# Weight pieces, chunk 1's twiddle terms and the transform lead in the early part of a fused FFT-filter and MoE kernel

## Chip, cores and metric

One NeuronCore of a Trainium2 chip runs the whole program in one launch. The metric is device time in microseconds (us) of an execution; lower is better. Engine names: PE is TensorE (matmuls), DVE is VectorE, ACT is ScalarE, POOL is GpSimd, SP is the SyncE queue that issues most DMAs.

## Reference

Three layers follow each other over a batch of 8 sequences of 3072 tokens with 256 channels. The spectrum filter acts along the sequence, the other two on each token.

```python
X = np.fft.rfft(x, axis=1); Y = X * (filt_r + 1j * filt_i)[None]
y = np.fft.irfft(Y, n=3072, axis=1)                    # (8, 3072, 256)
h = np.maximum(np.maximum(y @ w1, y @ w2), y @ w3)     # 256 -> 768
x = h @ w_out                                          # 768 -> 256
h = x @ w_in                                           # 256 -> 1024
e = exp(h - max(h)); solu = h * e / (sum(e) + 1e-09)
ln = (solu - mean) / sqrt(var + 1e-06) * g_ln
out = ln @ w_out2
```

## The kernel before

**Transforms.** The 8 sequences and two halves of the channels make 16 chunks (chunk = 2 x sequence + half). A chunk's 24 x 128 transform is a radix part on DVE (`dft8` L274, `fwd3` L337, and on the way back `inv3` L360, `idft8` L303) around four groups of 128-point products on PE (`prod`, L390, fp32). For a group `fwd_in` (L395) multiplies by twiddles into a tile U, `middle` (L444) makes the products in a PSUM pair `pf` and multiplies them by the filter on DVE (Y and M), and `inv_out` (L521) multiplies back, and ACT and DVE scale the result out of `pf` into the chunk's tile S (T by ACT, then `S<-pf,tws,T` by DVE). Chunks 0 to 3 use full products, later ones half products with two partition swaps by DMA. For chunks 0 and 1 (`apart`, L392) the two summands of each twiddle term are not added: ACT makes both, in U and in T, and PE sums them by two more products. For the later chunks ACT makes one summand and DVE adds the other: `stt(U[...], X[...], col("c", k), T[...])`, L419 and L438.

**Tiles.** Chunk tiles go round in five buffers with tags s0 to s4 (`take`, L257: `j = ch % NS`). Two of them first serve the weights: `w3f` holds w3 in tag s2, the buffer of chunk 2 (L142), and `raws` holds three incoming pieces in tag s4, the buffer of chunk 4 (L177).

**Weights of the MoE.** They arrive as float64 bits in 12 pieces (`PIECES`, L172: for each third of d_ff w3, w1, w2, w_out). `moe_weights` (L175) loads a piece by SP (L190), `from_f64` (L151) turns it into fp32 on DVE and ACT, w3 is subtracted from w1 and w2 (L198), and each weight is split in a high and a low part (L199, L200). Behind the last piece come six rounds (L203 to L215, transposes of `w3f` on PE, a copy on ACT, a subtraction on DVE L210, six products) that multiply w3 with w_out into `a_h`, `a_l` (L217, L218); this is called the fold here. They hold two of the four PSUM banks of tag h throughout.

**MoE steps.** A step `moe(i)` (L755) is one block of 128 hidden units for 512 tokens: `up` (L700) makes 12 products in two banks, ACT and DVE take the maximum (L710, L712) and split it (L715, L716), and `down` (L719) of two steps earlier adds 6 products into `o`. Six steps make a group of 512 tokens, closed by 12 products with `a_h`, `a_l` (L736); 36 steps make a sequence. A group's tokens come from the finished transform by a transpose on DVE and 16 SP DMAs (`flip`, L661, tiles yt and zt), then ACT and DVE split them (`xT`, L676, xh and xl). So the first group of a sequence needs both its chunks, and steps 37 and 73 are the first of the second and third sequence.

**What sets the order.** The program is written as generators: the transforms are one stream (`fft_stream`, L625), advanced by `advance()`, and the loop at L791 writes a step and then advances the stream up to a budget of DVE cost:

```python
while cost[0] - c0 < (i + 1) * PACE + LEAD * min(1.0, i / RAMP) and idle < 12:
```

The tile framework's scheduler then orders each engine's instructions from the written order. On the chip each engine runs its instructions in that order, and SP issues its DMAs in that order too, so that a row that waits holds up all rows behind it. The first loop (L773) advances the stream until a third of chunks 0 and 1 is back (Y), with a weight piece at every 20th advance for `EARLY` = 4 pieces; the other eight and the fold are written after step 0 (L794). `fft_stream` writes chunk 4's radix part (L645) only after chunk 3 is complete (L642).

From the seventh sequence on the program needs no transforms any more; the last sequence of the first MoE is mixed with the second MoE's first products, and then the second MoE runs alone to the end.

Of the kernel before, what the change touches and what calls it, by code (L numbers as in the profile page):

```python
# [10 lines left out]
F32 = mybir.dt.float32  # L11
# [8 lines left out]
P = 128  # L20
# [79 lines left out]
def kernel(ctx: ExitStack, tc: tile.TileContext, xr, ff, tw, dft,  # L100
                                 w1, w2, w3, w_out, w_in2, w_out2, g_ln, out):
    nc = tc.nc
    B = xr.shape[0]
    DFF = w1.shape[1]
    NF = DFF // P
# [19 lines left out]
    fc = fx.enter_context(tc.tile_pool(name="fc", bufs=1))  # L125
# [13 lines left out]
    w_h = [wp.tile([P, 2, DFF], F32R, tag=f"w{j}h", name=f"w{j}h") for j in range(2)]  # L139
    w_l = [wp.tile([P, 2, DFF], F32R, tag=f"w{j}l", name=f"w{j}l") for j in range(2)]  # L140

    w3f = fc.tile([P, 2, DFF], F32, tag="s2", name="w3f")  # L142
    a_h = wp.tile([P, 2, D], F32R, tag="ah", name="ah")
    a_l = wp.tile([P, 2, D], F32R, tag="al", name="al")
    wo_h = wp.tile([P, NF, D], F32R, tag="woh", name="woh")
# [5 lines left out]
    def from_f64(raw, e, out=None, eng=nc.gpsimd):  # L151

        lw, hw = raw[:, 0::2], raw[:, 1::2]
        lf, hf, ef = lw.bitcast(F32), hw.bitcast(F32), e.bitcast(F32)
        nc.vector.tensor_scalar(e, hw, 0x7FF00000, None, op0=ALU.bitwise_and)
        nc.scalar.activation(e, e, AF.Relu, bias=ebias, scale=8.0)
        nc.vector.tensor_scalar(lw, lw, 8, None, op0=ALU.logical_shift_right)
        nc.vector.scalar_tensor_tensor(e, hw, -2 ** 31, e, op0=ALU.bitwise_and, op1=ALU.bitwise_or)
        nc.vector.tensor_scalar(hw, hw, 0xFFFFF, None, op0=ALU.bitwise_and)
        nc.scalar.activation(hf, hw, AF.Copy, bias=1.0, scale=2.0 ** -20)  # L160
        nc.vector.scalar_tensor_tensor(lf, lw, 2.0 ** -44, hf, op0=ALU.mult, op1=ALU.add)
        if out is not None:
            ef, lf = (v.rearrange("p (c w) -> p c w", c=2) for v in (ef, lf))
            eng.tensor_tensor(out, ef, lf, op=ALU.mult)
            return e.bitcast(F32)
        eng.tensor_tensor(ef, ef, lf, op=ALU.mult)
        return ef
# [2 lines left out]


    PIECES = [(q, j) for q in range(NF // 2) for j in (2, 0, 1, 3)]  # L172
    EARLY = 4

    def moe_weights():  # L175

        raws = yp.tile([P, 3, 1024], I32, tag="s4", name="raws")  # L177
        for i, (q, j) in enumerate(PIECES):
# [11 lines left out]
            nc.sync.dma_start(raw.rearrange("p (c w) -> p c w", c=2), src.rearrange("(c p) w -> p c w", p=P))  # L190
            with tc.issue_after(GATE[0]) if i >= EARLY else nullcontext():
                v = from_f64(raw, e, w3f[:, :, fs] if j == 2 else None, nc.vector)
# [40 lines left out]
    FULL, SUMS = 4, 2  # L233
# [19 lines left out]
    def free(ch):  # L253

        return ch < NS or ((ch - NS) // 2, TG - 1) in FLIPPED
# [18 lines left out]
    def dft8(ch):  # L274
        take(ch)
        O = S[ch]
        scr = scratch()
        eo, f = by3(scr[:, 0:24]), by3(scr[:, 24:30])
        parts = [slice(a, a + 1) for a in range(3)] if ch == 0 else [slice(0, 3)]
        for a in parts:  # L280
            tt(eo[:, 0:4, a], O[:, 0:4, a], O[:, 4:8, a], ALU.add)
            yield
            tt(eo[:, 4:8, a], O[:, 0:4, a], O[:, 4:8, a], ALU.subtract)
            yield
        tt(f[:, 0:2], eo[:, 0:2], eo[:, 2:4], ALU.add)
        yield
        tt(O[:, 6:8], eo[:, 0:2], eo[:, 2:4], ALU.subtract)
        yield
        tt(O[:, 0], f[:, 0], f[:, 1], ALU.add)
        yield  # L290
        tt(O[:, 1], f[:, 0], f[:, 1], ALU.subtract)
        yield
        h = eo[:, 0:2]
        tt(h[:, 0], eo[:, 5], eo[:, 7], ALU.subtract)
        yield
        tt(h[:, 1], eo[:, 5], eo[:, 7], ALU.add)
        yield
        stt(O[:, 2:4], h, C8, eo[:, 4:8:2])
        yield
        stt(O[:, 4:6], h, -C8, eo[:, 4:8:2])  # L300
        yield
# [58 lines left out]
    def inv3(ch):  # L360
        v = S[ch]
        scr = scratch()
        s, d, t, t0 = scr[:, 0:6], scr[:, 6:12], scr[:, 12:18], scr[:, 18:20]
        tt(s, v[:, 2:8, 1], v[:, 2:8, 2], ALU.add)
        yield
        tt(d, v[:, 2:8, 1], v[:, 2:8, 2], ALU.subtract)
        yield
        stt(t, s, -0.5, v[:, 2:8, 0])
        yield
        tt(v[:, 2:8, 0], v[:, 2:8, 0], s, ALU.add)  # L370
        yield
        stt(v[:, 3:8:2, 1], d[:, 0:6:2], H3, t[:, 1:6:2])
        stt(v[:, 2:8:2, 2], d[:, 1:6:2], H3, t[:, 0:6:2])
        yield
        stt(v[:, 2:8:2, 1], d[:, 1:6:2], -H3, t[:, 0:6:2])
        stt(v[:, 3:8:2, 2], d[:, 0:6:2], -H3, t[:, 1:6:2])
        yield
        stt(t0, v[:, 0:2, 1], -0.5, v[:, 0:2, 0])
        tt(v[:, 0:2, 0], v[:, 0:2, 0], v[:, 0:2, 1], ALU.add)
        yield  # L380
        tt(v[:, 0:2, 1], t0, v[:, 0:2, 2], ALU.add)
        tt(v[:, 0:2, 2], t0, v[:, 0:2, 2], ALU.subtract)
        yield
# [6 lines left out]
        nc.tensor.matmul(o, m, rows(src, i0, i1), start=first, stop=last)  # L390

    def apart(ch, g):  # L392
        return ch < SUMS

    def fwd_in(ch, g):  # L395
        sl, ks = GROUPS[g]
# [182 lines left out]
    def together(*gens):  # L579
        gens = [g for g in gens if g is not None]  # L580
        while gens:
            for g in list(gens):
                try:
                    next(g)
                except StopIteration:
                    gens.remove(g)
                else:
                    yield

    def seq(*gens):  # L590
        for g in gens:
            yield from g

    def groups(ch, last=None):

        if last is None:
            yield from fwd_in(ch, 0)
        else:
            yield from together(fwd_in(ch, 0), last)
        yield from together(fwd_in(ch, 1), middle(ch, 0))  # L600
        yield from together(fwd_in(ch, 2), middle(ch, 1), inv_out(ch, 0))
        yield from together(fwd_in(ch, 3), middle(ch, 2), inv_out(ch, 1))

    def rest(ch):
        yield from together(middle(ch, 3), inv_out(ch, 2))
        yield from inv_out(ch, 3)

    def stages(before, ch):

        ready = ch is not None and free(ch)  # L610
        if ready:
            yield from dft8(ch)
        if before is not None:
            while before not in VDONE:
                yield
            yield from inv3(before)
            yield from idft8(before)
        if ch is not None:
            if not ready:
                while not free(ch):  # L620
                    yield
                yield from dft8(ch)
            yield from fwd3(ch)

    def fft_stream():  # L625

        one, two = slice(0, 1), slice(1, 3)
        yield from dft8(0)
        yield from fwd3(0)
        yield from together(groups(0), stages(None, 1))  # L630
        yield from together(groups(1, rest(0)), first(0, one))
        yield from rest(1)
        yield from first(1, one)
        yield from idft8(0, two)
        yield from idft8(1, two)
        last = 2 * B - 1
        if B > 1:

            yield from stages(None, 2)
            yield from together(groups(2), stages(None, 3))  # L640
            yield from together(groups(3, rest(2)), stages(2, None))
            yield from seq(rest(3), inv3(3), idft8(3))  # L642
        for ch in range(4, 2 * B):
            if ch == 4:
                yield from stages(None, 4)  # L645
            yield from together(groups(ch, rest(ch - 1) if ch > 4 else None),
                                stages(ch - 1 if ch > 4 else None, ch + 1 if ch < last else None))
        if B > 2:
            yield from seq(rest(last), inv3(last), idft8(last))

    def first(ch, part):
        while ch not in VDONE:
            yield
        yield from inv3(ch)
        yield from idft8(ch, part)
# [99 lines left out]
    def moe(i):  # L755
        b, tg, f = steps[i]
        up(b, tg, f)
        if i >= LD:
            down(*steps[i - LD])
        j = b * TG + tg + 1  # L760
        if f == XF and j < B * TG:
            xT(*divmod(j, TG))
        if f == FF and j < B * TG:
            have(*divmod(j, TG))
            flip(*divmod(j, TG))

    XF, FF = 4, 1
    wgen = moe_weights()
# [4 lines left out]
    while (0, 0, 0) not in Y or (0, 1, 0) not in Y:  # L773
        advance()
        n += 1
        if n == 1:
            nc.sync.dma_start(tws, tw)
            nc.sync.dma_start(dfull, dft[:, 4:14])
            nc.sync.dma_start(df, dft[:, 0:4])
        if n % NW0 == 0 and n <= EARLY * NW0:  # L780
            next(wgen)
# [4 lines left out]
    xT(0, 0)  # L786
    c0 = cost[0]

    PACE, LEAD, RAMP = 3080.0, 16000.0, 6
    n_a = (B - 1) * per  # L790
    for i in range(n_a):  # L791
        moe(i)
        b, tg, f = steps[i]
        if i == 0:  # L794
            for _ in wgen:
                pass
        idle, at = 0, cost[0]
        while cost[0] - c0 < (i + 1) * PACE + LEAD * min(1.0, i / RAMP) and idle < 12:
            if not advance():
                break  # L800
            idle, at = (0, cost[0]) if cost[0] > at else (idle + 1, at)
# [282 lines left out]
```

## Time and profile before

| | us |
|---|---|
| median of 3 runs (2787.57 to 2789.47) | 2788.5 |
| the profiled execution's own time | 2787.83 |
| its span in the trace | 2786.0 |
| PE busy, share of the span | 2675.1, 96% |
| DVE busy, share of the span | 2308.8, 83% |
| ACT busy | 1485.2, 53% |
| POOL busy | 905.9, 33% |

The profiled execution is 0.7 us below the median. Times in the trace count from the span's start, so 1.8 us of the execution lie around the span. Steps are told here by the start of their L712 on DVE: the n-th L712 is the n-th step.

### The profile page before, as it was taken

The page shows a single profiled execution, that of the slowest core. Times are in us where ns is not written, and L with a number is a line of the kernel's source. Part 1 is how long each engine was busy: PE and PEld are TensorE (multiplying, and loading weights), DVE is VectorE, ACT ScalarE, POOL GpSimd, SP SyncE. Part 2 cuts the span into 40 slices and gives each one's busy share as a digit, 9 for nine tenths or more (in the row PEclk, how much of TensorE's full clock was granted, in tenths as well). Part 3 has the DMA queues.
Part 4 walks back from the last instruction along what each step waited for, and adds up shares of the span by engine and source line. Part 5 has one row for each costly group of instructions (what it writes and reads, how often), then busy time and mean ns, then how long its engine had stood idle before and what let it go on. Part 6 is the DMA issues. An engine that isn't in the chain of part 4 may idle for free.

```text
span 2786.0 us, 37981 instructions
## 1 busy us (share of the span) xinstructions
PE 2675.1 (96%) x12008; PEld 2154.1 (77%) x12008; DVE 2308.8 (83%) x3962; ACT 1485.2 (53%) x2896; POOL 905.9 (33%) x1302
## 2 busy tenths in 40 slices
PE   6779979979999999999999999999999999999999
PEld 3457757757777777777778888888888888888888
DVE  8797699999799898998988635988878878778885
ACT  4244334434444444444434434777777777677775
POOL 0001101101111111111111101666767776766765
PEclk9889989989999999999999999999999999999999
DMA  4123113322323224223322312556555555555543
GB/s 165 40 93 101 37 37 82 114 60 76 104 78 101 83 73 119 61 71 99 84 70 80 95 31 61 145 134 159 143 141 138 144 146 142 150 145 138 144 125 91
DMA packets 162281, 285.58 MB, mean 103 GB/s; under 512 B 34464, under 2 KB 95392, under 8 KB 160160
## 3 DMA queue, kind: packets, MB, share of 16 engines
q1 hardware_dynamic: 121376, 232.82, 31.4%
q10 hardware_dynamic: 40704, 50.35, 5.5%
q8 instruction: 94, 1.54, 0.2%
q14 instruction: 107, 0.88, 0.1%
HBM read 89.04 MB, written 50.33 MB: 50 GB/s over the span
## 4 chain that ended last, share of the span: by engine, by line
PE 79%; DVE 15%; DMA 2%; issue 1%; SPq 1%; ACT 1%; POOL 0%; DVEq 0%; ACTq 0%; POOLq 0%
PE h L707 20%; PE h L885 19%; PE p L954 13%; PE pf L390 7%; PE p L956 7%; DVE scr L240 4%; PE o L736 4%; PE o L728 3%; PE o L729 3%; PE o L727 3%; DVE S L244 2%; DVE S L240 1%; DVE h L712 1%; DVE hl L716 1%; SPq L672 1%
## 5 line engine op out<-in xcount | busy, mean ns | idle before, releaser
L947 POOL TENSOR_TENSOR sl<-zt,sh 128x1024 fp32r<-128x1024 f32 x188 | 452.4, 2406 | 106.1 <-ACT sh L946 99.2
L954 PE MATMUL p<-V,sh 128*128 128x512 f32 x1536 | 380.9, 390 | 0.0
L896 DVE SCALAR_TENSOR_TENSOR sp<-h,e 128x1024 f32<-128x1024 f32 x192 | 234.3, 1220 | 172.1 <-ACT e L894 170.0
L240 POOL TENSOR_TENSOR M<-M,M 128x384 f32<-128x384 f32 (+1 forms) x96 | 134.4, 1420 | 685.0 <-DVE M L240 505.1
L715 ACT CAST hh<-h 128x512 fp32r<-128x512 f32 x288 | 169.3, 589 | 349.4 <-DVE h L712 336.7
L954 PEld LDWEIGHTS p<-V,sh 128*128 128x128 f32 x1536 | 287.5, 188 | 59.5
L710 ACT ACTIVATE hm<-h 128x512 f32<-128x512 f32 x288 | 172.9, 601 | 247.4 <-PE h L707 246.1
L894 ACT ACTIVATE e<-h,sm 128x1024 f32<-128x1024 f32 x192 | 213.7, 1113 | 107.5 <-DVE sm L892 61.4
L946 ACT CAST sh<-zt 128x1024 fp32r<-128x1024 f32 x188 | 196.6, 1047 | 117.9 <-PE p L954 94.3
L892 DVE TENSOR_REDUCE sm<-h 128x1 f32<-128x1024 f32 x192 | 230.9, 1203 | 28.0 <-PE h L885 27.4
L898 ACT ACTIVATE e<-sp,sm 128x1024 f32<-128x1024 f32 x192 | 220.5, 1149 | 55.1 <-DVE sm L900 54.0
L728 PE MATMUL o<-hl,woh 128*128 128x512 f32 x576 | 238.7, 414 | 9.7 <-DVE hl L716 9.4
L885 PE MATMUL h<-wih,x2h 128*128 128x512 f32 x768 | 244.0, 392 | 1.2 <-ACT xo L739 1.2
L712 DVE TENSOR_TENSOR h<-hm,h 128x512 f32<-128x512 f32 x288 | 197.3, 685 | 55.8 <-PE h L707 51.7
L885 PE MATMUL h<-wih,x2l 128*128 128x512 f32 x768 | 241.5, 391 | 0.0
L885 PE MATMUL h<-wil,x2h 128*128 128x512 f32 x768 | 238.2, 390 | 0.0
L913 DVE STREAM_TRANSPOSE yt<-sp 128x1024 f32<-128x1024 f32 x188 | 231.5, 1231 | 5.2 <-issue 1.0
L727 PE MATMUL o<-hh,woh 128*128 128x512 f32 x576 | 231.6, 402 | 3.3 <-ACT hh L715 3.3
L716 DVE TENSOR_TENSOR hl<-h,hh 128x512 fp32r<-128x512 f32 x288 | 195.7, 681 | 41.4 <-ACT hh L715 41.0
L729 PE MATMUL o<-hh,wol 128*128 128x512 f32 x576 | 226.7, 394 | 0.0
L956 PEld LDWEIGHTS p<-V,sl 128*128 128x128 f32 x1536 | 209.8, 190 | 15.0
L956 PE MATMUL p<-V,sl 128*128 128x256 f32 x1536 | 214.7, 282 | 0.0
(160 smaller groups left out, 5757.3 us busy)
## 6 DMA issues: line engine op xcount, KB each, us to landing
zt<-yt SPq DMA_DIRECT2D x752, 128.0 KB, 2.7
x<-xo SPq DMA_DIRECT2D x96, 256.0 KB, 2.2
x<-x ACTq DMA_DIRECT2D x48, 512.0 KB, 3.7
out_dram<-ob ACTq DMA_DIRECT2D x192, 128.0 KB, 2.3
zt<-yt SPq DMA_DIRECT2D x752, 32.0 KB, 1.9
S<-in_xr_dram SPq DMA_DIRECT2D x15, 1536.0 KB, 8.3
F<-in_ff_dram SPq DMA_DIRECT2D x48, 384.0 KB, 3.4
F<-in_ff_dram SPq DMA_DIRECT2D x16, 512.0 KB, 4.2
```

The costliest lines, as they stand in the source:

```text
L240: eng.tensor_tensor(o, a, b, op=op)
L707: nc.tensor.matmul(ph[j], wt[:, c, f * P:(f + 1) * P], xt[:, c], start=i == 0, stop=i == 5)
L727: nc.tensor.matmul(po[m], wo_h[:, f, cs], hh, start=f == 0, stop=False)
L728: nc.tensor.matmul(po[m], wo_h[:, f, cs], hl, start=False, stop=False)
L729: nc.tensor.matmul(po[m], wo_l[:, f, cs], hh, start=False, stop=False)
L885: nc.tensor.matmul(h[:, fs], xt[:, c, ts], wt[:, c, fs], start=n == 0, stop=n == 5)
L892: nc.vector.tensor_reduce(sm[:, 0:1], h, axis=AX.X, op=ALU.max, negate=True)
L896: nc.vector.scalar_tensor_tensor(sp, h, 1.0, e, op0=ALU.mult, op1=ALU.mult, accum_out=sm[:, 2:3])
L913: nc.vector.transpose(out=YT[g][:, :, t].rearrange("p j c k -> p c j k"), in_=sp.rearrange("p (c j k) -> p c j k", c=NF2, j=4))
L947: nc.gpsimd.tensor_tensor(lv, z, hv, op=ALU.subtract)
L954: nc.tensor.matmul(p, sh[:, c], V2[:, c], start=c == 0, stop=False)
L956: nc.tensor.matmul(p[:, :D], sl[:, c], V2[:, c, :D], start=False, stop=c == NF2 - 1)
```

## The change

Five things change. (1) `EARLY` is 8, so two thirds of w1, w2, w3 and w_out are written into the first loop. (2) After step 0 only the last four pieces are written, the fold is written after step 4 (`NF - 2`), and the transform stream is not advanced after steps 0 to 3. (3) `w3f` lies in chunk 3's buffer (s3) instead of chunk 2's. (4) `apart` holds for chunk 0 alone: chunk 1's twiddle terms are added on DVE, and its two further products per half fall away; chunk 1's way back keeps its sums on PE (`SUMS` is still 2). (5) Chunk 4's radix part is written beside chunk 3's groups, and the lead that the budget gives the transforms grows to 40000 over 24 steps instead of 16000 over 6.

```diff
-    w3f = fc.tile([P, 2, DFF], F32, tag="s2", name="w3f")
+    w3f = fc.tile([P, 2, DFF], F32, tag="s3", name="w3f")
...
-    EARLY = 4
+    EARLY = 8
...
     def apart(ch, g):
-        return ch < SUMS
+        return ch < 1
...
-            yield from together(groups(3, rest(2)), stages(2, None))
+            nxt = stages(None, 4) if B > 2 else None
+            yield from together(groups(3, rest(2)), seq(stages(2, None), nxt or ()))
             yield from seq(rest(3), inv3(3), idft8(3))
         for ch in range(4, 2 * B):
-            if ch == 4:
-                yield from stages(None, 4)
...
-    PACE, LEAD, RAMP = 3080.0, 16000.0, 6
+    PACE, LEAD, RAMP = 3080.0, 40000.0, 24
...
         if i == 0:
+            for _ in range(EARLY, len(PIECES)):
+                next(wgen)
+        if i == NF - 2:
             for _ in wgen:
                 pass
+        if i < 4:
+
+            continue
```

Lines behind L393 of the kernel before are one lower in the changed kernel up to the new lines in `fft_stream` and the loop. In names of the order below a number tells buffers apart: S_148 is chunk 0, S_197 chunk 1.

**Place 1, DVE, middle of the first transforms (about 54 to 64 us in the trace before).** `we` and `raws` belong to weight pieces, `U` are twiddle terms. Before:

```order
L244 SCALAR_TENSOR_TENSOR S_148<-pf_274,tws_131,T2_300 128x2x128 x3
L159 TENSOR_SCALAR raws_179<-raws_179 128x512
L244 SCALAR_TENSOR_TENSOR S_148<-pf_337,tws_131,T2_361 128x2x128 x3
L161 SCALAR_TENSOR_TENSOR raws_179<-raws_179 128x512
L166 TENSOR_TENSOR we_377<-we_377,raws_179 128x512
L240 TENSOR_TENSOR Y_415<-pf_391,F_389 128x1024
L240 TENSOR_TENSOR M2_416<-pf_391,F_389 128x1024
```

And now:

```order
L244 SCALAR_TENSOR_TENSOR S_148<-pf_274,tws_131,T2_300 128x2x128 x3
L244 SCALAR_TENSOR_TENSOR U_372<-S_197,tws_131,T_373 128x2x128 x2
L155 TENSOR_SCALAR we_427<-raws_179 128x512
L244 SCALAR_TENSOR_TENSOR U_372<-S_197,tws_131,T_373 128x2x128
L159 TENSOR_SCALAR raws_179<-raws_179 128x512
L244 SCALAR_TENSOR_TENSOR S_148<-pf_337,tws_131,T2_361 128x2x128 x3
L158 SCALAR_TENSOR_TENSOR we_427<-raws_179,we_427 128x512
L244 SCALAR_TENSOR_TENSOR U_460<-S_197,tws_131,T_461 128x2x128
L240 TENSOR_TENSOR Y_415<-pf_395,F_393 128x1024
L240 TENSOR_TENSOR M2_416<-pf_395,F_393 128x1024
```

Chunk 1's terms and the fifth piece (`we_427`) stand between chunk 0's results; both were absent there.

**Place 2, SP, the loads of chunks 2 to 4 (about 150 to 180 us).** Before, S_998 is chunk 2 and S_2308 chunk 4 (chunk 3's load stands near the start):

```order
L190 DMA raws_179<-in_w2_dram 128x2x512
L672 DMA zt_1226<-yt_1225 32x256 x7
L190 DMA raws_179<-in_w_out_dram 128x2x512
L672 DMA zt_1226<-yt_1225 32x256 x4
L266 DMA S_998<-in_xr_dram 128x3072
L266 DMA S_2308<-in_xr_dram 128x3072
L740 DMA x2_0_60<-xo_1219 128x512
```

Now, S_1788 is chunk 4 and S_1129 chunk 3 (chunk 2's load stands near the start):

```order
L190 DMA raws_179<-in_w_out_dram 128x2x512
L671 DMA zt_825<-yt_824 32x256
L671 DMA zt_1182<-yt_1181 32x256 x16
L266 DMA S_1788<-in_xr_dram 128x3072
L266 DMA S_1129<-in_xr_dram 128x3072
L463 DMA F_1304<-in_ff_dram 128x768
L739 DMA x2_0_60<-xo_1175 128x512
```

The late load is now chunk 3's; the filter rows F_1304 of chunk 2's second group stand behind it.

**Place 3, DVE, before the third sequence (steps 67 to 72, about 580 us).** The flip that starts it is `yt_4253<-S_2515` before and `yt_4270<-S_2237` now. Before, from the L712 of step 72 on:

```order
L712 TENSOR_TENSOR h_4362<-hm_4375,h_4362 128x512
L240 TENSOR_TENSOR M1_4200<-Z_4188,F_4131 128x768
L240 TENSOR_TENSOR scr_4205<-scr_4205 128x384 x2
L240 TENSOR_TENSOR S_2515<-scr_4205 128x2x384 x2
L240 TENSOR_TENSOR M2_4189<-swap_4193,F_4131 128x768
L244 SCALAR_TENSOR_TENSOR U_4600<-S_3043,tws_131,T_4601 128x128 x4
L716 TENSOR_TENSOR hl_4379<-h_4362,hh_4378 128x512
L244 SCALAR_TENSOR_TENSOR S_2515<-scr_4205 128x2x384 x2
L668 STREAM_TRANSPOSE yt_4253<-S_2515 128x4x4x32
```

Now, from the L711 (L712 before) of step 67 on:

```order
L711 TENSOR_TENSOR h_4184<-hm_4197,h_4184 128x512
L715 TENSOR_TENSOR hl_4161<-h_4144,hh_4160 128x512
L667 STREAM_TRANSPOSE yt_4270<-S_2237 128x4x4x32
L244 SCALAR_TENSOR_TENSOR Z_4056<-pf_3949,tws_131,M2_4057 128x384
L244 SCALAR_TENSOR_TENSOR Z_4056<-M2_4057,tws_131,pf_3949 128x384
L240 TENSOR_TENSOR scr_4075<-S_4073 128x1536 x2
L244 SCALAR_TENSOR_TENSOR EO_3905<-swap_3900,tws_131,M1_3865 128x384
L244 SCALAR_TENSOR_TENSOR EO_3905<-M1_3865,tws_131,swap_3900 128x384
L711 TENSOR_TENSOR h_4226<-hm_4239,h_4226 128x512
```

The flip stood behind step 72 and now stands behind step 67; the `xl` of that group is behind step 70.

## Rows read from the trace of the kernel before

**Rows 1.** Page, part 2: busy tenths in 40 slices of 69.65 us.
```profile
PE   6779979979999999999999999999999999999999
PEclk9889989989999999999999999999999999999999
```

**Rows 2.** Table by stretch: length, PE, PEld, DVE, ACT, POOL busy (instructions), PEclk, DMA.
```profile
52.84:122.59 69.75, 61.51 (x187) 35.27 (x186) 47.14 (x95) 23.22 (x77) 0.20 (x1) 0.95 0.16 45
122.59:205.68 83.09, 58.10 (x226) 45.30 (x225) 79.47 (x142) 32.67 (x61) 0.00 (x0) 0.74 0.28 89
205.68:366.95 161.27, 161.27 (x647) 121.35 (x646) 118.44 (x186) 63.68 (x159) 20.00 (x18) 1.00 0.20 64
366.95:391.05 24.10, 6.70 (x30) 5.22 (x28) 23.93 (x33) 2.33 (x5) 0.00 (x0) 0.72 0.15 44
391.05:396.05 5.00, 5.00 (x14) 4.03 (x15) 5.00 (x10) 2.08 (x5) 0.00 (x0) 0.62 0.01 2
400.00:460.00 60.00, 56.88 (x237) 43.74 (x236) 60.00 (x98) 31.18 (x77) 7.13 (x7) 1.00 0.28 74
581.13:653.25 72.12, 57.41 (x214) 42.71 (x213) 69.19 (x105) 29.21 (x71) 11.36 (x9) 0.88 0.31 84
700.00:1000.00 300.00, 292.48 (x1221) 228.05 (x1220) 273.51 (x443) 133.09 (x315) 34.94 (x27) 1.00 0.31 89
1000.00:1650.00 650.00, 646.25 (x2742) 513.79 (x2741) 549.14 (x900) 287.78 (x646) 81.23 (x69) 1.00 0.28 81
```

**Rows 3.** Waits of DVE, 53 to 123 us: in total, times, longest; then its timeline's end.
```profile
DVE S L244 <- ACT T L560: 12.6, 5, 3.7
DVE Y L240 <- PE pf L390: 7.5, 2, 4.7
...
122.59 0.42 DVE L155 TENSOR_SCALAR we<-raws 128x512 int32<-128x512 int32 x1
```

**Rows 4.** Timeline of DVE, rows of a weight piece: start, us, what.
```profile
165.47 0.69 DVE L198 TENSOR_TENSOR we<-we,w3f 128x512 f32<-128x512 f32 x1
166.07 0.42 DVE L157 TENSOR_SCALAR raws<-raws 128x512 int32<-128x512 int32 x1
166.41 0.42 DVE L159 TENSOR_SCALAR raws<-raws 128x512 int32<-128x512 int32 x1
```

**Rows 5.** Timelines of DVE and POOL, twiddle terms beside POOL and without it; [idle before].
```profile
217.33 2.40 DVE L244 SCALAR_TENSOR_TENSOR U<-S,tws,T 128x256 f32<-128x256 f32 x2
396.50 0.87 DVE L244 SCALAR_TENSOR_TENSOR U<-S,tws,T 128x256 f32<-128x256 f32 x2
...
215.83 3.62 POOL L240 TENSOR_TENSOR Y<-Y,M 128x384 f32<-128x384 f32 x2 [136.19 <-DVE M L240]
```

**Rows 6.** Groups of PE by shape, 26 to 112 us: busy us, mean ns; then its timeline.
```profile
L390 PE MATMUL pf<-T,dfull 128*128 128x384 f32 x48 | 18.1, 495 | 0.0
...
116.46 1.09 PE L691 MATMUL h<-ident,S 128*128 128x128 f32 x4 [4.07 <-DVE S L244]
```

**Rows 7.** Chunk loads between 150 and 200 us: time to landing.
```profile
DMA to landing us min/median/max: 6.5/7.4/8.3
```

**Rows 8.** Timeline of DVE: the second sequence's flip, and step 72.
```profile
378.02 0.70 DVE L668 STREAM_TRANSPOSE yt<-S 128x512 f32<-128x512 f32 x1
...
581.13 0.69 DVE L712 TENSOR_TENSOR h<-hm,h 128x512 f32<-128x512 f32 x1
```

**Rows 9.** Timelines of SP (one flip's issues), ACT and PE at the second sequence's start.
```profile
205.39 10.02 SPq L672 DMA_DIRECT2D zt<-yt  x16
...
390.38 1.14 ACT L685 CAST xh<-zt 128x512 fp32r<-128x512 f32 x2 [15.62 <-DMA zt<-yt]
...
391.05 0.80 PE L707 MATMUL h<-xh,w0h 128*128 128x512 f32 x1 [17.41 <-ACT xh L685]
```

**Rows 10.** Timeline of PE around the third sequence's start.
```profile
589.41 0.79 PE L728 MATMUL o<-hl,woh 128*128 128x512 f32 x1 [6.42 <-DVE hl L716]
...
601.81 2.90 PE L390 MATMUL pf<-U,df 128*128 128x384 f32 x4 [5.38 <-DVE S L244]
```

## The prediction

> **What bounds the kernel now.** I first read the slices of the page [rows 1]. From the eleventh slice (about 700 us) on PE and its clock stand at 9, and the table by stretch [rows 2] gives the price of what is left there: between 1000 and 1650 us PE is busy 646.25 of 650.00 at a granted clock of 1.00. PE is the bound there, the change takes nothing from its work there, so I expect nothing from that part. The loss lies earlier, in four places [rows 2], whose first ends are the starts of steps 9 and 36 (205.68, 366.95), of PE's work on the second sequence (391.05), and of steps 72 and 81.
> - 122.59 to 205.68 (weights and fold): PE is busy 58.10 of 83.09 us at a clock of 0.74, DVE 79.47. DVE bounds it.
> - 366.95 to 391.05 (the step from the first to the second sequence): PE busy 6.70 at 0.72, which is 4.8 us of work at full clock, so 19.3 lost, and 5.00 x 0.38 = 1.9 more at half clock just behind.
> - 581.13 to 653.25 (nine steps from the 72nd, where the third sequence begins): 57.41 at 0.88 is 50.5 us of work in 72.12, so 21.6 lost, 14.7 of it idle. The idle times are a wait for DVE in the first steps, not for the clock [rows 10].
> - 400 to 460: 3.1 us lost, with DVE busy all 60.00; 700 to 1000: 7.5.
>
> Before them DVE also sets the pace, but not alone: from 52.84 to 122.59 it is busy 47.14 of 69.75 us [rows 2] and else waits, 12.6 us for ACT's T and 7.5 for PE's products [rows 3]. 122.59 is the first row of the fifth weight piece [rows 3], the end of chunks 0 and 1's first third; I call it T0. So in this stretch DVE has 22.6 us in which work can be put, and behind T0 it has 3.6. That is what the change acts on.
>
> All sums below stand against the profiled execution, 2787.83 us, 0.7 below the median. What a measurement of this kernel can tell from no change is about 0.2%, 5.6 us.
>
> **Start to T0: -3.** Four weight pieces come in ahead. A row of a piece starts 0.60 us behind one of the longer kind and 0.34 behind one of the shorter [rows 4]. A piece has three short rows and 3, 5, 5 and 4 long ones (w3, w1, w2, w_out), so 2.8 + 4.0 + 4.0 + 3.4 = 14.3 us. Chunk 1's terms bring 13 additions, nine of 256 columns at 0.87 / 2 = 0.435 [rows 5] and four half as wide at 0.22: 4.8. 47.1 + 14.3 + 4.8 = 66.2 against 69.75; half a us of wait remains, so -3. PE loses the T products of chunk 1, 24 of the 48 rows, 9 us [rows 6]; DVE is then the bound here, so they count nothing. Ends: -5.5 (2 us of the pieces slip into waits ahead of 52.84) and +3 (6.5 of the 20 us of ACT and PE waits can't be filled, since the rows stand in order).
>
> The 13 additions might cost more. Beside POOL's Y the same two terms took 2.40 us against 0.87 alone [rows 5], 0.77 more each. In my stretch POOL is busy 0.20 of 69.75 us [rows 2], and at 215.83 it had idled for 136.19 [rows 5]; so I take 0.435. The Trainium skill, "SBUF — State Buffer", section "SBUF: two separate sides", speaks against moving additions to DVE: VectorE with two SBUF inputs and GpSimd hold one pair of ports as an exclusive lock, for a whole instruction. The trace agrees where both run, and by that rule with POOL busy throughout, the terms would cost some 8 us more and the sum below would come to -25.
>
> **T0 to step 9: -1.** Four pieces fewer (-14.3). Instead radix work on chunks 2 and 3 stands there that stood later; the rows of DVE up to step 9, by these spacings, come to 4.8 less in all. Against that, chunk 3's load (place 2) now waits for the last reader of `w3f`, which is the fold's transposes; SP takes its rows in order, so the filter rows F_1304, the stores of x2 and the next flip's zt queue behind it, and DVE's first radix row of chunk 3 waits for it. Such loads took 6.5 to 8.3 us to land [rows 7]; DVE has other rows for about half, so +3, with ends of 0 and 8.3. The fold now runs between steps, its ping-pong of PE, ACT and DVE +1. Ends: -5 and +4.
>
> **Step 9 to 36: -2.3.** PE is busy 161.27 of 161.27 us at full clock, DVE 118.44 [rows 2]: what DVE gains in rows is hidden, DVE has 43 us of cover. PE's rows between these steps come to 1.0 us less, and one of chunk 4's product groups lies ahead already (-1.3). Ends -2.3 and 0.
>
> **Step 36 to the second sequence: -6.9.** Now 24.1 us pass between step 36 and PE's restart [rows 2]: 11.1 to the flip [rows 8], then 13.0 for 16 DMA issues (10 us of them on SP), the landing and ACT's first xh; PE waited 17.41 for that [rows 9]. This chain is not cut by the change, chunk 3 still ends last. But fewer rows stand between step 36 and the flip (8.2 us by their spacings), -3. And three product groups of chunk 4 stand there on PE, each four rows of the kind that took 2.90 at half clock [rows 10], so 1.3 to 1.45 at full: -3.9, work that was done later before. So the stall shrinks and stays. Ends: -8.2 and -3.9 (the groups' inputs come late).
>
> **Step 72: -20.** Place 3 of the order: the flip of the third sequence stood behind step 72 and now stands behind step 67, its xl behind step 70. A step is 50.5 / 9 = 5.6 us of PE work, three steps are 16.8, and from flip to PE 13.0 are needed [rows 8, 9]; so it is hidden. Of the 21.6 us lost I take 20, since one late xl may stay. The first of the two idle times, 6.42 behind DVE's hl [rows 10], goes as well, because the rows of the way back no longer crowd between L712 and hl. Ends: -21.6, and -14.7, only the idle share.
>
> The price of this is DVE's load. Between steps 36 and 72 its rows come to 192.7 us and PE's to 189.3; some 20 of DVE's lie in the gap at step 36, where PE waits anyway, so 172 stand beside about 180. In 700 to 1000 us DVE was busy 273.51 of 300.00 [rows 2]. It fits, barely. What lost 3.1 us in 400 to 460 stays.
>
> Sum: -3 - 1 - 2.3 - 6.9 - 20 = -33.2, so 2787.83 - 33.2 = 2754.6. All best ends, with the 5 us that a longer lead could save of the small losses up to 1000 us, are -48, **2740**; all worst ends +3 + 4 + 0 - 3.9 - 14.7 = -11.6, 2776.
>
> **Rivals.**
> - *A, the stall of step 72 moves.* DVE, at over 95% from step 36 on, falls behind and the flip comes at the same time, only at another step. For: DVE was busy 69.19 of 72.12 us in the stretch after step 72 [rows 2]. Against: the flip has five steps' head start. It gives -13.2, **2774.6**.
> - *B, slower: the lead starves the steps.* A longer lead puts rows of transforms ahead of hl and h on DVE, which runs in order; PE then waits a little in every step as in 400 to 460, where 3.12 of 60.00 us were lost, 5.2%, with DVE full. Over 400 to 1500 us that is 57, less the 14 that are lost there now: -33 + 43 = +10, **2798**. It decides from a loss of (33 + 14) / 1100 = 4.3% on. Against: the rows of the transforms are no more in sum, and 581 to 653 is the only stretch behind 400 where PE lost more than that.
> - *C, no change.* The pieces don't fit into DVE's waits and T0 comes 5 us late; DVE stands for chunk 3's load in full (+8); the stall at step 36 grows by the same DVE work, since PE's cover is used up, and the flip of step 72 moves by these. What is left of -33 is within 5 us: **2788**. For: the order sums say DVE has 28 us more to do up to step 36 than before. Against: 43 us of cover between steps 9 and 36.
> - That the change does not do what it says is excluded: the order shows all five parts.
>
> **Chances.** The forecast 0.73 (its own range 2742 to 2766: step 72 freed in whole or part), A 0.14, B 0.07, C 0.06. A and the forecast are faster by over 0.2%, 0.87; C is no change, 0.06; B is slower, 0.07. The range takes in the forecast's bounds and A: 2738 to 2778; outside lie B, C and some 0.05 of the forecast.
>
> **What would show it.** In the changed kernel's trace: T0's counterpart, step 1's rows, about 3 us earlier; step 9 at about 202, with a wait of DVE for chunk 3's load of 0 to 8 us; step 36 at 359 to 361; PE's restart on the second sequence about 381, with PE still idle for about 10 us before it and half clock behind; no PE wait over 3 us and a clock of 1.00 near the 72nd step, about 565; DVE fuller than before between 400 and 560. Wrong would be: PE idle time scattered at 0.2 us and more per step between 400 and 1000 us (B), an idle stretch near step 72 of over 6 us (A), or step 36 later than 367 (C).

## The result, and the profile after

The changed kernel takes 2758.66 us (median of 4 runs, 2756.94 to 2760.07) against 2788.03 for the kernel before; the ratio is 0.9895, interval 0.9883 to 0.9908. That is 29.4 us faster, 4 us less than the 33.2 forecast, and inside the forecast's own range. The profiled execution took 2758.79 us with a span of 2757.0, 29.0 less than before; the numbers below stand against that.

The slices of the page of the changed kernel, busy tenths in 40 slices of 68.9 us, answer to [rows 1]:

```profile
PE   6879979999999999999999999999999999999999
...
PEclk9889989999999999999999999999999999999999
```

The 7 of PE's ninth slice is gone and so is the 8 of the granted clock there; the 7 and the 8 of the sixth stand. For the sizes, the table by stretch of the changed kernel (length, then PE, PEld, DVE, ACT and POOL busy with their instructions, clock, DMA share, GB/s):

```profile
0.00:205.00 205.00, 149.05 (x503) 96.70 (x504) 196.85 (x354) 80.84 (x208) 6.12 (x13) 0.91 0.33 107
205.00:360.00 155.00, 153.78 (x617) 115.56 (x615) 125.98 (x197) 64.51 (x164) 18.28 (x14) 1.00 0.18 60
360.00:420.00 60.00, 46.77 (x166) 34.04 (x167) 59.97 (x89) 22.17 (x54) 10.77 (x6) 0.86 0.29 76
420.00:560.00 140.00, 139.25 (x585) 109.42 (x584) 132.39 (x218) 62.27 (x151) 18.04 (x15) 1.00 0.32 93
560.00:640.00 80.00, 79.25 (x334) 62.32 (x333) 77.79 (x129) 36.94 (x88) 9.85 (x9) 1.00 0.26 69
...
700.00:1300.00 600.00, 588.16 (x2449) 458.91 (x2447) 573.95 (x923) 267.60 (x640) 71.19 (x59) 1.00 0.29 83
1300.00:1800.00 500.00, 496.50 (x2205) 405.24 (x2206) 345.03 (x592) 237.62 (x445) 106.34 (x164) 1.00 0.29 81
```

and the same stretches of the kernel before:

```profile
0.00:205.00 205.00, 145.61 (x484) 95.63 (x485) 172.52 (x307) 79.10 (x198) 1.09 (x8) 0.88 0.31 101
205.00:360.00 155.00, 155.00 (x624) 117.17 (x623) 113.17 (x174) 60.93 (x151) 20.00 (x18) 1.00 0.21 67
360.00:420.00 60.00, 41.40 (x162) 31.19 (x162) 58.84 (x92) 21.39 (x53) 1.27 (x3) 0.86 0.14 35
420.00:560.00 140.00, 137.95 (x576) 107.66 (x575) 137.61 (x224) 66.29 (x161) 22.55 (x16) 1.00 0.34 98
560.00:640.00 80.00, 65.29 (x245) 48.33 (x244) 74.85 (x121) 31.97 (x81) 8.11 (x7) 0.89 0.24 64
...
700.00:1300.00 600.00, 588.86 (x2458) 459.82 (x2457) 554.83 (x895) 269.76 (x642) 71.21 (x57) 1.00 0.31 89
1300.00:1800.00 500.00, 498.70 (x2192) 405.84 (x2191) 364.95 (x620) 232.79 (x454) 94.08 (x137) 1.00 0.28 79
```

What PE loses in a stretch is its length less busy time x clock. The first row of after gives 205 - 149.05 x 0.91 = 69.4 us, of before 76.9: 7.5 gained. Down the rows the loss goes from 0 to 1.2, from 24.4 to 19.8, from 2.1 to 0.8, from 21.9 to 0.8, from 11.1 to 11.8 and from 1.3 to 3.5. The sum goes from 137.7 to 107.3, 30.4 less, beside the 29.0 of the spans. As PEclk has two digits, one of the first rows is good to 0.7 us, and a long row at 1.00 can't show a change of the work by a few us. By this measure the loss shrinks in three places, 21.1 us near step 72, 7.5 in the start and 4.6 around step 36, and behind 700 us it grows by 2.9.

That 30.4 lies near 29.0 is no check of these sizes. First, the mean clock of a stretch is low mostly from time in which PE has nothing to do, so the measure asks too much where PE stands idle at half clock. Around step 36 before, with the stretch cut where the granted clock changes, the rows are

```profile
360.00:377.78 17.78, 13.65 (x55) 9.97 (x54) 16.68 (x30) 4.41 (x11) 0.00 (x0) 1.00 0.08 30
377.78:394.84 17.06, 3.79 (x9) 3.05 (x10) 16.99 (x25) 2.35 (x5) 0.00 (x0) 0.50 0.13 31
394.84:420.00 25.16, 23.97 (x99) 18.17 (x99) 25.16 (x39) 14.64 (x37) 1.27 (x3) 1.00 0.18 41
```

and PE's work is 13.65 + 3.79 x 0.50 + 23.97 = 39.5 us, so 20.5 lost and not 24.4. Cut in this way, the start, step 36 and step 72 lose 71.6, 20.5 and 20.0 us before and 64.7, 19.4 and 0.7 now. Second, PE has less to do: part 1 of the pages counts 11976 products for 12008 and 2665.9 us of busy time for 2675.1, since the change takes 32 products of chunk 1 away. So only the 19 to 21 us near step 72 are a firm size; step 36 gives between 1 and 5, and the start about 7 beside the products that it no longer makes.

PE's timeline in the changed kernel at these places (start, us, what, idle before):

```profile
120.88 0.79 PE L706 MATMUL h<-xh,w0h 128*128 128x512 f32 x1 [0.90 <-ACT xh L691]
...
365.68 0.79 PE L727 MATMUL o<-hl,woh 128*128 128x512 f32 x1 [6.44 <-DVE hl L715]
...
377.33 2.90 PE L390 MATMUL pf<-U,df 128*128 128x384 f32 x4 [4.46 <-DVE S L244]
380.30 0.79 PE L706 MATMUL h<-xh,w0h 128*128 128x512 f32 x1
...
407.60 3.35 PE L390 MATMUL pf<-U,df 128*128 128x512 f32 x4 [2.96 <-DVE S L244]
```

The row before that answers to the first is

```profile
124.96 0.79 PE L707 MATMUL h<-xh,w0h 128*128 128x512 f32 x1 [0.85 <-ACT xh L692]
```

so PE's token products come 4.1 us earlier. The second sequence starts at 380.30, before at 391.05 [rows 9], with 6.44 and 4.46 us of idle time ahead of it and products at 0.6 us (half clock) behind each; no idle time over 3 us is left near step 72. On DVE the rows of steps 9 and 36, the flips of the second and third sequence, and DVE's wait for chunk 3's load between 100 and 240 us (total, times, longest) are:

```profile
194.38 0.68 DVE L711 TENSOR_TENSOR h<-hm,h 128x512 f32<-128x512 f32 x1
...
357.38 0.69 DVE L711 TENSOR_TENSOR h<-hm,h 128x512 f32<-128x512 f32 x1
...
367.28 0.70 DVE L667 STREAM_TRANSPOSE yt<-S 128x512 f32<-128x512 f32 x1
...
545.79 0.69 DVE L667 STREAM_TRANSPOSE yt<-S 128x512 f32<-128x512 f32 x1
```

```profile
DVE scr L240 <- DMA S<-in_xr_dram: 0.3, 1, 0.3
```

From flip to PE 13.0 us pass, as before (380.30 - 367.28), and the load that moved behind the fold costs 0.3 us. Step 9 comes 11.3 us earlier and step 36 9.6. The flip of the third sequence, which was

```profile
591.01 0.70 DVE L668 STREAM_TRANSPOSE yt<-S 128x512 f32<-128x512 f32 x1
```

before, comes 45 us earlier.

### The profile page after: what moved, and what is told of

Its sections match the earlier page's. It is cut to its first block, busy times and chain, and to the rows that moved or that the text cites. A ratio compares the mean times of both kernels' runs of the same rounds, so it can differ in the third digit from the quotient of the medians.

```text
span 2757.0 us, 37909 instructions
## 1 busy us (share of the span) xinstructions
PE 2665.9 (97%) x11976; PEld 2144.8 (78%) x11976; DVE 2315.4 (84%) x3975; ACT 1477.0 (54%) x2883; POOL 904.9 (33%) x1302
## 3 DMA queue, kind: packets, MB, share of 16 engines
q1 hardware_dynamic: 121376, 232.82, 31.7%
## 4 chain that ended last, share of the span: by engine, by line
PE 69%; DVE 11%; DMA 2%; issue 2%; SPq 1%; ACT 1%; POOL 0%; DVEq 0%; ACTq 0%; POOLq 0%
PE h L890 19%; PE h L706 16%; PE p L959 13%; PE p L961 7%; PE pf L390 3%; PE o L735 3%; PE o L727 3%; PE o L728 3%; PE o L726 3%; DVE scr L240 2%; SPq L671 1%; DVE S L244 1%; DVE h L711 1%; DVE hl L715 1%; DVE S L240 1%
## 5 line engine op out<-in xcount | busy, mean ns | idle before, releaser
L727 PE MATMUL o<-hl,woh 128*128 128x512 f32 x576 | 238.1, 413 | 11.6 <-DVE hl L715 11.4
L711 DVE TENSOR_TENSOR h<-hm,h 128x512 f32<-128x512 f32 x288 | 196.4, 683 | 53.1 <-PE h L706 48.0
```

Of the source, the lines that this page charges most:

```text
L711: nc.vector.tensor_tensor(ph[1], hm, ph[1], op=ALU.max)
L727: nc.tensor.matmul(po[m], wo_h[:, f, cs], hl, start=False, stop=False)
```

## The experiments

The first theory was that of the prediction: the wait at a sequence's start is set by where its flip stands in DVE's order. All runs compute the whole output. After each stand the median and the ratio to the kernel before, run beside it (there 2786.8 to 2788.6 us, so a difference from the first row can be 1 us off); "loss" is PE's by the mean clock, as above, in the three stretches 0 to 205, 360 to 420 and 560 to 640 us. Where PE idles at half clock it is too large, in these runs by up to 6.5 us in the first stretch and by up to 4.6 in the others.

| kernel | us | ratio, interval | loss in the three |
|---|---|---|---|
| before | 2788.0 | 1 | 76.9, 24.4, 21.9 |
| lead alone | 2789.0 | 1.0003, 0.9994 to 1.0012 | 77.0, 23.9, 17.5 |
| chunk 4 alone | 2782.0 | 0.9980, 0.9971 to 0.9989 | 76.5, 31.2, 6.5 |
| 8 pieces alone | 2772.3 | 0.9942, 0.9929 to 0.9956 | 58.6, 23.8, 20.9 |
| late fold alone | 2792.7 | 1.0017, 1.0008 to 1.0026 | 87.9, 0.7, 34.3 |
| weight parts alone | 2773.8 | 0.9955, 0.9942 to 0.9967 | 68.1, 5.8, 30.5 |
| changed, chunk 4 back | 2772.0 | 0.9941, 0.9927 to 0.9955 | 69.0, 7.6, 31.7 |
| changed, lead back | 2760.0 | 0.9899, 0.9886 to 0.9913 | 68.2, 17.4, 9.5 |
| changed | 2758.7 | 0.9895, 0.9883 to 0.9908 | 69.4, 19.8, 0.8 |
| changed, terms back | 2753.4 | 0.9877, 0.9864 to 0.9891 | 67.8, 11.6, 2.1 |
| changed, 7 pieces | 2752.5 | 0.9876, 0.9861 to 0.9891 | 74.4, 12.1, 2.1 |
| changed, 6 pieces | 2750.4 | 0.9867, 0.9854 to 0.9881 | 81.6, 2.5, 5.5 |
| changed, 4 pieces | 2759.8 | 0.9898, 0.9885 to 0.9912 | 88.1, 2.2, 5.5 |
| changed, 6 pieces, terms back | 2760.3 | 0.9905, 0.9889 to 0.9922 | 81.7, 4.4, 0.8 |

**The lead.** Lengthened alone on the kernel before (the diff shown), and put back in the changed one (the reverse):

```diff
-    PACE, LEAD, RAMP = 3080.0, 16000.0, 6
+    PACE, LEAD, RAMP = 3080.0, 40000.0, 24
```

> The kernel before with one edit, the lead of 40000 over 24 steps. The order of DVE still has the flip of the third sequence behind step 72 (step 36 for the second). My theory (the time at step 72 is decided by where that flip stands in DVE's order, and the longer lead alone doesn't move it): the stall of 21.6 us stays, 2788 us, within 4 us of the kernel before. Rival (the longer lead alone frees the stall, the other parts give the rest): about 2768 us.

> The changed kernel with the lead put back to 16000 over 6 steps. The flip of the third sequence stands behind step 71 in DVE's order, one step ahead where 13 us are needed and a step gives 5.6. My theory: some 13 to 16 of the 19.5 us come back as a stall near step 72, 2772 to 2775 us. Rival (the early pieces and chunk 4's earlier radix part free the stall, the lead does nothing): 2759 us, within 3 us of the changed kernel.

Alone it does nothing; put back it costs 1.4 us, within the intervals. The stretch near step 72 is, with the lead put back (first) and with the lead alone (second),

```profile
560.00:640.00 80.00, 71.95 (x292) 55.10 (x291) 75.02 (x120) 34.58 (x83) 9.18 (x7) 0.98 0.28 76
```

```profile
560.00:640.00 80.00, 66.46 (x248) 47.94 (x248) 78.13 (x126) 31.85 (x83) 9.34 (x7) 0.94 0.24 65
```

With the lead put back it loses 9.5 us, 8.7 more than in the changed kernel and not 13 to 16 more, and other stretches lose less (17.4 for 19.8 at step 36). The first theory held for the first run and fell in the second: counting the steps between a flip and its use, at 5.6 us each against 13 us to cover, gave too long a wait, and the total hardly moved. So the longer lead gives no time of its own that these runs can show.

**Chunk 4's radix part.** Taken back in the changed kernel; then alone on the kernel before (the same lines with - and + exchanged):

```diff
-            nxt = stages(None, 4) if B > 2 else None
-            yield from together(groups(3, rest(2)), seq(stages(2, None), nxt or ()))
+            yield from together(groups(3, rest(2)), stages(2, None))
...
+            if ch == 4:
+                yield from stages(None, 4)
```

> The changed kernel with chunk 4's radix part back in its old place, behind chunk 3; the long lead stays. The flip of the third sequence stands behind step 72 in DVE's order. My theory: the stall near step 72 is back in full, +20, and the three product groups of chunk 4 that covered the wait at step 36 are gone, +4: 2779 to 2783 us. Rival (the lead frees the stall, chunk 4's place is only 4 us worth): 2763 us.

> The kernel before with one edit: chunk 4's radix part beside chunk 3's groups. Theory now: this part, and not the lead, takes the stall near step 72 away (in the run without it the stretch 560 to 620 lost 28 us, in the changed kernel 0.8), and it costs some 6 us before 420 us, since its rows stand ahead of the flip of the second sequence. So -20 +6: about 2775 us, and PE loses under 8 us between 560 and 640. Rival (it pays only with the room that the early weight pieces made on DVE): 2785 to 2789 us, the stall near step 72 still 15 us or more.

Taken back it costs 13.3 us. The rows of that run in the table by stretch, and from PE's timeline its longest wait there, which the changed kernel doesn't have:

```profile
360.00:420.00 60.00, 55.70 (x223) 43.77 (x224) 59.93 (x96) 28.04 (x70) 5.22 (x5) 0.94 0.25 69
...
560.00:640.00 80.00, 55.47 (x200) 38.84 (x200) 80.00 (x123) 30.40 (x77) 13.25 (x9) 0.87 0.29 76
```

```profile
573.33 2.90 PE L390 MATMUL pf<-EO,df 128*128 128x384 f32 x4 [11.33 <-DVE EO L244]
```

Near step 72 PE loses 31.7 us instead of 0.8, but only 7.6 instead of 19.8 at step 36. So this part takes 30.9 away there and puts 12.2 in at step 36: its rows stand on DVE ahead of the second flip, which comes at 367.28 with it and came at 355.50 without. Alone it does the same in small:

```profile
360.00:420.00 60.00, 37.46 (x125) 25.18 (x124) 58.11 (x88) 17.55 (x47) 5.16 (x5) 0.77 0.20 52
...
560.00:640.00 80.00, 75.03 (x307) 57.94 (x306) 75.50 (x127) 35.91 (x89) 6.16 (x7) 0.98 0.25 68
```

PE loses 15.4 us less near step 72 and 6.8 more at step 36, and the median is 5.7 us below that of the kernel before run beside it. Both runs lie between the two forecasts written for them: the places are right, and the price at step 36 is near the 6 us written for the second run and twice that in the changed kernel.

**Weight parts.** All of them on the kernel before (8 pieces, four behind step 0, fold behind step 4, no transforms behind steps 0 to 3, w3f in s3); then the same with 4 pieces, called the late fold alone, though the pacing of steps 0 to 3 and w3f's place go with it; then 8 pieces alone, whose whole edit is

```diff
-    EARLY = 4
+    EARLY = 8
```

> The kernel before with the weight parts alone: eight pieces in the first loop, four behind step 0, the fold behind step 4, no transforms behind steps 0 to 3, w3f in chunk 3's buffer. Chunk 1's terms stay on PE and ACT, chunk 4 and the lead as before. Theory: DVE bounds until step 9, so these parts give what the run without chunk 4's part gave, -16, less nothing or up to 3 more since DVE has 4.8 us fewer rows: 2769 to 2773 us. Rival (the 9 us of PE work of chunk 1's second products count in full): 2779 to 2782 us.

> The run of the weight parts alone (2773.8 us) with 4 weight pieces ahead in place of 8: so the kernel before with the fold behind step 4, no transforms behind steps 0 to 3, and w3f in chunk 3's buffer, eight pieces behind step 0. Theory (the pieces save 14 to 19 us at the start, and only 5.8 us of wait at step 36 was left to clear in that run): the start loses about 14 to 19 again and the wait gives 4 back, 2783 to 2789 us, so the gain of the weight parts is the pieces'. Rival (the later fold gives the gain, as it lets steps 1 to 4 and the transforms through): 2772 to 2777 us.

> The kernel before with 8 weight pieces ahead in place of 4 and nothing else; the fold stays behind step 0. Theory (the pieces fill waits of DVE up to 123 us and give the gain of the weight parts): 2773 to 2778 us. Rival (the second sequence's flip stands behind step 36 as before, so what the start gains shows as a longer wait there): 2784 to 2789 us.

The pieces alone give 15.5 us, more than the weight parts together; the late fold alone is 4.9 us slower. The rows of the run with the pieces alone:

```profile
0.00:205.00 205.00, 157.39 (x540) 104.08 (x541) 186.74 (x332) 87.08 (x220) 3.37 (x10) 0.93 0.32 105
...
360.00:420.00 60.00, 42.10 (x166) 32.10 (x165) 59.93 (x92) 24.30 (x60) 3.17 (x3) 0.86 0.20 52
...
560.00:640.00 80.00, 66.40 (x245) 49.55 (x244) 75.31 (x113) 31.48 (x77) 11.84 (x9) 0.89 0.29 77
```

18.3 us come out of the start alone, and both later waits stand as before (16.00 and 6.43 us of idle time, against 17.41 [rows 9] and 6.42 [rows 10]). The rival, that they only move the gain into the wait at step 36, falls: the flip comes sooner too (363.44 for 378.02). With the late fold alone:

```profile
0.00:205.00 205.00, 133.08 (x379) 79.17 (x380) 173.89 (x309) 76.79 (x204) 5.97 (x13) 0.88 0.29 91
...
360.00:420.00 60.00, 59.31 (x258) 48.11 (x258) 59.21 (x89) 26.23 (x58) 0.21 (x1) 1.00 0.16 44
...
560.00:640.00 80.00, 57.82 (x203) 41.58 (x202) 74.94 (x120) 28.86 (x76) 8.90 (x9) 0.79 0.24 63
```

the wait at step 36 is gone, and the start loses 11.0 and the stretch near step 72 12.4 more: fewer steps are done ahead of the second flip, so PE has work there, and none is won.

**Chunk 1's terms.** Back on PE and ACT in the changed kernel:

```diff
-        return ch < 1
+        return ch < SUMS
```

> The changed kernel with chunk 1's twiddle terms back on PE and ACT (two summands, two more products per half). Theory: DVE has 4.8 us fewer rows before its first third is done and PE 9 us more work there, beside which it has idle time; the second sequence's flip comes up to 4 us sooner: 2755 to 2759 us. Rival (PE's 9 us count in full, since PE's work bounds the whole): 2767 us.

```profile
0.00:205.00 205.00, 149.15 (x487) 94.92 (x488) 184.81 (x330) 82.86 (x218) 5.62 (x13) 0.92 0.31 102
...
360.00:420.00 60.00, 51.52 (x201) 37.63 (x200) 60.00 (x90) 24.42 (x60) 8.48 (x7) 0.94 0.27 71
```

The kernel is five us faster without this part, though the intervals overlap (the runs do not: 2751.3 to 2754.5 against 2756.9 to 2760.1): beside 8 pieces and the late fold, the move to DVE costs time. How is not shown. DVE is busy 184.81 instead of 196.85 us up to 205, but step 36 comes 17 us later in this run (374.31), while its flip comes only 2 us later (369.33); so more of the steps are left to fill the wait, and the loss around step 36 shrinks by 8.2 us. Far behind, from 700 us on, 5.6 us less are lost as well:

```profile
700.00:1300.00 600.00, 592.21 (x2473) 463.00 (x2472) 589.21 (x950) 270.27 (x647) 77.98 (x61) 1.00 0.30 85
1300.00:1800.00 500.00, 498.08 (x2228) 408.78 (x2227) 333.92 (x574) 241.44 (x445) 108.19 (x168) 1.00 0.29 80
```

In all stretches together PE loses 14.7 us less, and it makes the 32 further products, an estimated 9 to 11 us (18.1 / 2 for those of 384 columns [rows 6], and up to 2 for the rest). What is left agrees with the 5.3 measured.

**The number of pieces.** In the changed kernel 4, 6 and 7 in place of 8, and 6 with the terms back:

> The changed kernel with 4 weight pieces ahead instead of 8 (the other eight are written after step 0, the fold after step 4 as in the change). In DVE's order the flip of the second sequence stands behind step 32 instead of 36. My theory (the place of a flip decides the wait at a sequence's start): the wait at step 36 goes, some -15, and the start loses the 6 us of the early pieces or up to 12: 2750 to 2756 us. Rival (the early pieces are worth what they were meant for, since until step 9 DVE bounds, and PE's wait at step 36 only moves): 2765 to 2770 us.

> The changed kernel with 6 weight pieces ahead. With 4 the start lost 20 us more than with 8 and the wait at step 36, 20 us, was gone; the total was the same. Theory (what PE loses up to 420 us is set by DVE's and the transforms' chain up to the second sequence's flip, wherever the wait shows): start and step 36 share it, the total stays within 4 us of 2759. Rival (a middle count leaves less wait in both places): 2748 to 2753 us.

> The changed kernel with 7 weight pieces ahead. The flip stands behind step 35 as against 36 with 8 pieces and 32 with 6. Theory (the wait at step 36 goes by the flip's place in steps, the start by the pieces; half of each is taken): between the runs with 8 and 6 pieces, 2752 to 2756 us, some 10 us lost between 360 and 420. Rival (a whole piece less is enough to clear the wait, and the start loses 5 us less than with 6): 2746 to 2749 us.

> The changed kernel with 6 weight pieces ahead and chunk 1's twiddle terms back on PE and ACT. In DVE's order the flip of the second sequence stands behind step 30. Theory (DVE's rows up to the second sequence's flip are the bound, so what leaves DVE is gained until the wait at step 36 is zero; with 6 pieces only 2.5 us of loss were left there between 360 and 420): the two gains overlap, the 5 us of the terms come from the start alone, 2745 to 2749 us. Rival (with no wait left at step 36 PE's 9 us of extra products count): 2753 to 2759 us.

With 4 and 6 pieces the start and step 36 read (first fence 4, second 6):

```profile
0.00:205.00 205.00, 132.87 (x392) 79.38 (x392) 181.44 (x329) 75.49 (x201) 7.91 (x15) 0.88 0.30 97
...
360.00:420.00 60.00, 57.81 (x242) 44.87 (x242) 60.00 (x92) 26.36 (x64) 6.82 (x5) 1.00 0.29 80
```

```profile
0.00:205.00 205.00, 138.68 (x449) 86.04 (x450) 189.08 (x339) 78.59 (x209) 10.42 (x15) 0.89 0.32 104
...
360.00:420.00 60.00, 57.52 (x238) 44.09 (x238) 60.00 (x93) 28.11 (x70) 7.80 (x6) 1.00 0.28 75
```

From 4 to 8 pieces the start gains 18.7 us and step 36 gives 17.6 back: the same total. With 6 the start has 6.5 of the gain (11.6 of 22.0 with the stretch cut where the clock changes) and step 36 still loses little, so the sum is least; the theory that the total is fixed falls. Six pieces is the fastest kernel measured, 2750.4 us, its interval clear of the changed one; six and seven can't be told apart. Six pieces with the terms back expected both gains and got neither: PE's loss in the first two stretches is 86.1 against 84.1, and nothing pays for the 9 us of further products: 9.9 us are lost in the median. Where PE's wait at step 36 is gone, PE's work counts, and the part that cost 5 us beside 8 pieces gains 10 beside 6.

**Against the ranges written ahead.** Inside lie the lead alone and 7 pieces (by the theory), the lead put back and 6 pieces (by the rival). Chunk 4 alone, chunk 4 back and 4 pieces fell between their two ranges. The weight parts came out 0.8 us and the late fold 3.7 above the theory's range, 8 pieces alone 0.7 and the terms back 1.6 below it, and 6 pieces with the terms back 1.3 above the rival's.

## Why the prediction was right, and where not

- *Start to T0, and T0 to step 9 (-3, -1):* PE's first token product came 4.1 us sooner, and 7.5 us less were lost up to 205. The wait for chunk 3's load, set at 3, measured 0.3. The term that was mis-sized lies behind T0: step 9 came 11.3 us earlier where the two terms give 4, since I set the 14.3 us that leave DVE against radix work drawn ahead. The runs separate them: the pieces alone won 18.3 us of the start, and the late fold with its pacing took 9.5 back (58.6 to 68.1).
- *The terms (4.8 us on DVE, PE's 9 us count nothing):* the price of the rows was right: the 13 additions take 5.2 us in the changed kernel's trace, at 0.47 or 0.48 where one of 256 columns stands alone. POOL was busy 0.20 us from 50 to 82, where they stand. The Trainium skill's rule on the shared ports ("SBUF — State Buffer", section "SBUF: two separate sides") would have cost some 8 us more with POOL busy throughout, and no run here puts it to that test. That taking the terms back won 5.3 us, near this price, is luck: PE then had some 9 us more to do and lost 14.7 less. PE's 9 us leave out part of what falls away, since they are 24 of the 32 products. That they count nothing no run separates with 8 pieces, and with 6 it failed.
- *Step 9 to 36 (-2.3):* it went the other way. From step 9 to step 36 161.3 us passed before [rows 2] and 163.0 now (357.38 - 194.38), 1.7 more.
- *Step 36 (-6.9):* the restart was forecast at 381 with about 10 us of idle time, and came at 380.30 with 10.9. That it fits is partly luck: up to step 9 the kernel won 7 us more than forecast, and on the rest of the way it fell about as much short. From step 36 to the restart 22.9 us pass for 24.1. And between 360 and 420 the gain was at most 4.6, as a third wait of 2.96 stands at 407.60. And the sign of chunk 4's part was wrong here: I booked its products as 3.9 us of cover, while its rows on DVE hold up the flip and the run without it loses 12.2 less.
- *Step 72 (-20):* 21.1 measured. The step from order to time was right in size; its reason holds for chunk 4's part, as both runs on it show, and not for the lead, which I had taken along with it as the price of the gain. Between 400 and 560 DVE was to be fuller and was less busy, 152.39 us for 157.61.
- *Rivals:* A and C are out. B's mechanism may show a trace: 700 to 1800 us lost 15.3 instead of 12.4 us (12.5 with the lead put back), 2.9 more, against the 43 that it would take, and the sum had nothing for it.
- *What lies between 33.2 and 29.0:* up to the restart of the second sequence 10.75 us were won, about the 10 forecast; behind it 18.2 instead of some 23. The shorter gain lies there, though near step 72 alone the full 20 came: the third wait at 407.60 and the loss behind 700 us are 5.9 us against it. How far each of them counts, and what the 3.9 us of chunk 4's work done ahead gave, no run separates.

What stays open: which of the late fold, the pacing of steps 0 to 3 and w3f's place costs the 1.5 us that separate the weight parts from the pieces alone (the ratios overlap), and whether 8 pieces with the early fold and chunk 4's part beat 2750 us; neither was tried. Nor is it shown by which rows the terms on DVE cost 5 us beside 8 pieces and gain 10 beside 6.

## What to carry to other kernels

Two waits along one chain are not two terms of a sum: work taken from the start can come back as a wait at the next boundary (18.7 won, 17.6 given back), so change one quantity in steps and look for the point at which the second wait just vanishes. Read for each moved row on an in-order engine both what it lets through later and what it holds up where it now stands; chunk 4's part won 30.9 us at one boundary and cost 12.2 at the one before. A part with a sound reason should still be taken out once alone: here one of five cost 5 us, and another gave nothing. And a part's sign can hang on the others: the one that cost 5 us gained 10 with 6 pieces.

## What was not expected of the hardware

The half clock behind a wait did not grow with the wait. In the changed kernel's PE timeline

```profile
369.58 0.63 PE L735 MATMUL o<-xh,al 128*128 128x512 f32 x2
...
383.02 0.44 PE L706 MATMUL h<-xh,w0h 128*128 128x512 f32 x1
```

are the first rows at full spacing again (the two of the first row take 0.47 us up to the next row; a pair at half clock takes 0.85). So behind 6.44 us of idle time PE's products ran 3.9 us at half clock, from 365.68, and behind the shorter 4.46 us 5.7, from 377.33. The granted clock itself stood at its lower level, 0.50, equally long both times:

```profile
362.62:369.44 6.82, 3.76 (x9) 2.99 (x10) 6.82 (x11) 0.48 (x1) 1.99 (x2) 0.50 0.33 91
376.27:383.10 6.83, 5.70 (x11) 3.39 (x12) 6.80 (x13) 1.14 (x2) 0.00 (x0) 0.50 0.44 129
```

The first time it had fallen 3.1 us before PE had work again, the second time 1.1 us before. What passed at the lower level while PE still waited cost nothing, and only the rest slowed its products.
